# One transformer-like block on one core: seven block products in three of four token chunks, four of them summed by TensorE onto banks already read, and low parts of the probabilities on GpSimd

## The chip, the core and the metric

The kernel runs on one core of a Trainium2 chip. Its engines are TensorE (PE in the profile, with its weight loads as PEld), VectorE (DVE), ScalarE (ACT), GpSimd (POOL) and SyncE (SP), which issues the DMAs. The metric is device time in microseconds, the median over several runs of the program. Three runs of the kernel before took 1616.49, 1615.18 and 1614.28 us; the median is 1615.18 us.

## The reference

```python
x = A_x                                  # 1 x 2048 x 576
xn = _layernorm(x)
qkv = xn @ wqkv                          # 32 heads of 18; sliding window of 256 keys
p = softmax(mask(q @ k.T * 18 ** -0.5))
s = (p @ v) @ wo
g = silu(((xn @ w_gate) * (xn @ w_up)) @ w_down)    # 576 -> 4608 -> 576
return x + s * g
```

Everything is float32. The kernel keeps that precision by writing each number as a high and a low part in float16 and adding three products (high by high, high by low, low by high) for each wanted one.

## The kernel before, in words

**Stages.** A first stage normalizes x, turns it into XT (features on partitions, tokens along the free side: four blocks of 128 features and a tail of 64, each with high and low part), and computes q, k and v. The rest is one long loop of 72 slots (lines 1210 to 1232). A slot is a pair (g, c): g is one of 18 groups of 256 of the 4608 hidden features, c one of four chunks of 512 tokens, and c is the inner index. So chunk 2 comes in slots 2, 6, 10 and so on to 70. A slot does the gate and up products of its group for its chunk. Beside that, slot b carries one attention step s = b - 1 (64 steps: four chunks by sixteen pairs of heads), and the down projection of the slot before.

**Order.** A slot has 16 places. `at(slot, place, f, ...)` (line 547) writes a piece of work into a place, and `at_place` (550) issues it after the matmuls of that place. A place above 15 falls into the next slot. Every engine runs its own instructions in the order of issue, so the order is written out by hand. At one place score products come first, then the down projection, then all else in the order in which it was put there.

**A dense slot** (lines 1215 to 1231; chunks 2 and 3 before) does 13 passes of 512 tokens for each of four weight tiles `UW[g, k]` (52 matmuls at L1223) and two pairs of half passes (L1226, L1227) into the two PSUM banks named `up`. ACT copies the gate result out (`gate_out`, 922), DVE multiplies the up result with it into `ht` (`up_out`, 927).

**A seven slot** (chunks 0 and 1 before; `SEVEN`, line 418) splits the 2 x 2 x 2 block product of its tokens, features and inner blocks into seven products of half size instead of eight, in the manner of Strassen and Winograd. Products of sums need the sums of the weights (`t_sum`, 425, with `t_hi` and `t_lo`, 437 and 443: tiles `tf` and `tw`) and of the activations (`s_steps`, 451, made once for each chunk: tiles `sx`, `xd`, and one block of XT rewritten in place). `seven_place` (1060) issues 96 matmuls of 256 tokens (L1075), `SEVEN_N` (1117) of them in each place, and `seven_half` (1025) four half ones (L1031, L1033). Each product q gets a fresh `up` bank, of which there are two. `seven_read` (1089) reads a finished product: products 0, 3 and 4 are copied out by ACT (`seven_copy`, L1043), products 1, 2, 5 and 6 are read by DVE with an addition of an earlier sum (`seven_add`, L1047), three additions of two SBUF tiles go to POOL (`seven_sum`, L1051), and four multiplications of gate by up halves (`seven_mult`, L1057) go three to POOL and one to DVE.

**After the products**, in both kinds, ACT and DVE split `ht` into the high and low parts `hh` (`h_hi`, L934; `h_lo`, L939). The second `h_lo` comes at place 19 after a dense slot and at 21 after a seven slot, which are places 3 and 5 of the next one; the first comes at place 11 and at place 17. `down` (942) starts at place 7 of the next slot: eight rounds of six matmuls (L952) into the one bank `dn`, each added to `acc` by DVE (L957). Of the six, the last reads the low part of the second tile.

**Attention**: scores in PSUM (L826), row maximum and mask on DVE (L834, tile `sm`, four buffers), ACT shifts, exponentiates and casts the high part of P (L840, L844, L847), and `turn_probs` (852) subtracts to get the low part (L855). For the second head of a pair (j = 1) POOL does it; for the first head it is DVE, but in seven slots POOL does the blocks i = 1 and 3 (`PL_AT`, 850). Then SP issues a DMA that transposes P (L858, tile `pt`), and TensorE multiplies it with v (`weigh`, L867), seven to nine places later.

**Weights** of the next group are split in chunks 2 and 3 of this one and in chunk 0 of the next: `hi` on ACT (L152) and `lo` on DVE (L155), down weights also on POOL (L526).

## Time and profile before

| what | value |
|---|---|
| runs, median (lowest to highest) | 1615.18 us (1614.28 to 1616.49) |
| profiled execution: span from its first to its last instruction | 1611.0 us |
| granted TensorE clock in it | 1.000 |
| busy: DVE, ACT, POOL | 80%, 69%, 51% of the span |
| DMA queue of SP: share of 16 DMA engines | 63.7% |

Of the profiled execution the page gives the span and nothing around it. The median of the runs is 4.2 us above that span, which is start and end of the program. The profile has a page (busy time, slices of time, queues, the chain of work that ended last, the costliest groups of instructions) and views that answer questions: the waits, the chain piece by piece, the timeline, and busy times in windows. A row of the timeline is start, duration, engine, line, operation and tiles, and in brackets the idle time before it with what ended it. Matmul rows overlap, since matmuls are pipelined; the chain's rows do not.

### The profile page before, as it was taken

The numbers are of one execution on the slowest core, as the hardware profiler recorded it, in microseconds if no ns is written. First come the engines' busy times: TensorE is split into PE (matmuls) and PEld (weight loads), VectorE is DVE, ScalarE is ACT, GpSimd is POOL, SyncE is SP. The second block draws the span as 40 slices with busy tenths as digits, with TensorE's granted clock in tenths as the row PEclk, the third lists the DMA queues.
The fourth block names the chain that finished last, engine by engine and source line by source line (L and its number), as shares of the span: only waits on it lengthen the run. The fifth ranks groups of instructions, "written<-read, shape, count | busy, mean of one in ns | idle before, by whom it ended". The sixth has DMA issues, their size and how long they took to land.

```text
span 1611.0 us, 37834 instructions
## 1 busy us (share of the span) xinstructions
PE 1600.1 (99%) x13914; PEld 1086.2 (67%) x13914; DVE 1285.6 (80%) x3129; ACT 1117.7 (69%) x2211; POOL 827.5 (51%) x969
## 2 busy tenths in 40 slices
PE   8999999999999999999999999999999999999999
PEld 5464668576767676666767676767585757676677
DVE  7535788888888989898989898888888888976545
ACT  6433587878787878787878888887878787842230
POOL 3114456564746565656666656556565647453100
PEclk9999999999999999999999999999999999999999
DMA  9562445475656687777768686767686858660328
GB/s 237 172 188 88 128 83 126 95 130 97 130 107 127 134 135 132 128 142 124 151 117 151 111 157 112 152 113 153 112 155 114 156 116 152 118 132 1 61 74 221
DMA packets 548682, 206.70 MB, mean 128 GB/s; under 512 B 489360, under 2 KB 529296, under 8 KB 548496
## 3 DMA queue, kind: packets, MB, share of 16 engines
q1 hardware_dynamic: 548496, 204.28, 63.7%
q8 instruction: 109, 1.79, 0.5%
q14 instruction: 77, 0.63, 0.1%
HBM read 76.63 MB, written 23.75 MB: 62 GB/s over the span
## 4 chain that ended last, share of the span: by engine, by line
PE 96%; DMA 1%; DVE 1%; issue 1%; ACT 1%; SPq 0%; POOL 0%; POOLq 0%; DVEq 0%; ACTq 0%
PE up L1223 25%; PE dn L952 25%; PE up L1075 23%; PE pv L867 4%; PE s L342 3%; PE s L826 3%; PE s L952 2%; PE s L1185 2%; PE up L1185 1%; PE up L1226 1%; PE up L342 1%; PE s L293 1%; PE dn L342 1%; PE pv L342 1%; PE up L1031 1%
## 5 line engine op out<-in xcount | busy, mean ns | idle before, releaser
L952 PE MATMUL dn<-dnw,hh 128*128 128x288 f16 x3168 | 475.7, 286 | 0.0
L1223 PE MATMUL up<-XT,upw 128*128 128x512 f16 x1872 | 463.9, 378 | 0.0
L952 PEld LDWEIGHTS <-hh 128*128 128x128 f16 x3456 | 326.5, 98 | 155.5 <-issue 41.2
L957 DVE SCALAR_TENSOR_TENSOR acc<-dn,sc,acc 128x288 f32<-128x288 f32 x496 | 254.5, 513 | 146.0 <-PE dn L952 142.1
L840 ACT ACTIVATE mx<-mx,sig 128x1 f32<-128x1 f32 x512 | 193.3, 383 | 150.3 <-DVE mx L834 144.0
L1223 PEld LDWEIGHTS <-upw 128*128 128x128 f16 x1872 | 165.7, 97 | 138.7
L1075 PEld LDWEIGHTS <-upw 128*128 128x128 f16 x1728 | 163.8, 97 | 22.2 <-issue 1.1
L1075 PEld LDWEIGHTS <-tw 128*128 128x128 f16 x1728 | 156.4, 97 | 18.6 <-issue 1.1
L867 PEld LDWEIGHTS <-pt 128*128 128x128 f16 x2880 | 137.7, 96 | 38.1 <-DMA pt<-pp 0.4
L1075 PE MATMUL up<-XT,upw 128*128 128x256 f16 x1152 | 158.8, 272 | 0.5 <-DVE gt L1047 0.5
L1051 POOL TENSOR_TENSOR gt<-gt 128x512 f32<-128x512 f32 x108 | 137.9, 1277 | 15.7 <-ACT gt L1043 12.7
L867 PE MATMUL pv<-vt,pt 128*128 128x37 f16 x2880 | 142.9, 179 | 0.0
L934 ACT ACTIVATE hh<-ht 128x512 f16<-128x512 f32 x144 | 89.1, 619 | 76.4 <-POOL ht L1057 51.5
L886 POOL CAST ob<-o 128x144 f16<-128x144 f32 x64 | 19.5, 304 | 214.0 <-DVE o L882 214.0
L1075 PE MATMUL up<-sx,tw 128*128 128x256 f16 x864 | 126.4, 271 | 0.4 <-ACT gt L1043 0.4
L939 DVE SCALAR_TENSOR_TENSOR hh<-hh,ht 128x512 f16<-128x512 f16 x144 | 108.4, 753 | 13.9 <-ACT hh L934 13.0
L1075 PE MATMUL up<-XT,tw 128*128 128x256 f16 x864 | 111.7, 272 | 0.2 <-DVE gt L1047 0.2
L1047 DVE SCALAR_TENSOR_TENSOR gt<-up,gt 128x512 f32<-128x512 f32 x144 | 98.4, 683 | 6.1 <-PE up L1075 4.3
L1057 POOL TENSOR_TENSOR ht<-gt 128x256 f32<-128x256 f32 x108 | 89.9, 846 | 20.6 <-DVE gt L1047 17.7
L1043 ACT ACTIVATE gt<-up 128x512 f32<-128x512 f32 x108 | 63.0, 583 | 33.1 <-PE up L1075 25.6
L380 DVE TENSOR_REDUCE am<-raw 128x1 f32<-128x640 f32 (+1 forms) x108 | 83.9, 789 | 2.2 <-DMA raw<-in_B_w_gate_dram 1.6
L435 POOL TENSOR_TENSOR tf<-raw 128x256 f32<-128x256 f32 x72 | 68.7, 954 | 14.8 <-issue 7.4
(2289 smaller groups left out, 3035.5 us busy)
## 6 DMA issues: line engine op xcount, KB each, us to landing
raw<-in_B_w_down_dram SPq DMA_DIRECT2D x36, 288.0 KB
qk_d<-qp SPq DMA_DIRECT2D x18, 512.0 KB
raw<-in_B_w_gate_dram SPq DMA_DIRECT2D x36, 256.0 KB
raw<-in_B_w_up_dram SPq DMA_DIRECT2D x36, 256.0 KB
vt<-v_d SPq DMA_DIRECT2D x48, 111.0 KB
ks<-qk_d SPq DMA_DIRECT2D x96, 54.0 KB
v_d<-vo SPq DMA_DIRECT2D x16, 296.0 KB
xr<-in_A_x_dram SPq DMA_DIRECT2D x16, 288.0 KB
```

What stands on the lines that cost most here:

```text
L342: nc.tensor.matmul(ps, a, b, start=i == 0 and not opened, stop=i == 12 and opened)
L840: nc.scalar.activation(mx[:, 1:2], mx[:, 0:1], AF.Identity, bias=sig[:, 2:3], scale=sig[:, 1:2])
L867: nc.tensor.matmul(PVB[s][:, j, i, :VW], pt[:, 2 * nb * j + n], VT[s][:, lo_ + n % nb, j * VW:(j + 1) * VW], start=n == 0, stop=n == 2 * n ...
L934: nc.scalar.activation(hh[:, 0], h, AF.Copy, scale=1.0 / LO)
L939: nc.vector.scalar_tensor_tensor(hh[:, 1], hh[:, 0], -LO, h, op0=OP.mult, op1=OP.add)
L952: nc.tensor.matmul(ps[:, :HALF], a, b, start=q == 0, stop=q == len(l) - 1)
L957: nc.vector.scalar_tensor_tensor(d, ps[:, :HALF], SC[g][:, 9:10], d, op0=OP.mult, op1=OP.add)
L1047: nc.vector.scalar_tensor_tensor(seven_new(sl, name), CH[q], H_SC, x, op0=OP.mult, op1=OP.add)
L1051: nc.gpsimd.tensor_tensor(seven_new(sl, name), x, y, op=OP.add)
L1057: eng.tensor_tensor(HT[sl, f][:, 256 * i:256 * i + 256], u[:, 0:256], u[:, 256:512], op=OP.mult)
L1075: nc.tensor.matmul(CH[q][:, o], a, b, start=CH["n"] == 0, stop=last and q != 4)
L1223: nc.tensor.matmul(banks[up], a, b, start=i == 0 and not up, stop=i == 12 and up == 1)
```

## The change

- `SEVEN` becomes (0, 1, 2): chunk 2 goes from dense to seven slots, and gets its activation sums at places -10 to 14 around slot 0. Chunk 3 stays dense.
- The seven products come in the order 0, 2, 1, 3, 4, 5, 6. Products 1, 3, 5 and 6 get no fresh bank: TensorE adds them onto the bank of 0, 2, 3 and 4, after that bank has been read (`start=False`). What POOL's `seven_sum` added before is so added in PSUM, and `seven_sum` goes.
- The reads are now two copies by ACT (0 and 1) and five additions by DVE.
- `PL_AT` is (0, 1, 2, 3) in seven slots: POOL makes all low parts of P there.
- `t_hi` of the first two weight sums moves from place 45 to 47 and the first `t_lo` from 47 to 48, counted from the slot of chunk 0 of the group before.
- Since places of `h_hi`, `h_lo` and `score` depend on the kind of slot, chunk 2 now has those of a seven slot.

```diff
-    SEVEN = (0, 1)
+    SEVEN = (0, 1, 2)
...
+               (-10, -10, -9, -8, -6, -5, -4, 3, 4, 5, 6, 7, 8, 9, 10, 11, 13))
+    SUMS_ON = ("vvvvppvpvvpppvvvp", "ppppvpvpvvppvpvpv", "ppvvvpvpvvvpvpvpv")
...
-    PL_AT = ((), (1, 3))
+    PL_AT = ((), (0, 1, 2, 3))
...
-                at(b, (45, 45, 52, 57)[n], t_hi, g, n // 2, n % 2)
-                at(b, (47, 49, 56, 58)[n], t_lo, g, n // 2, n % 2)
+                at(b, (47, 47, 52, 57)[n], t_hi, g, n // 2, n % 2)
+                at(b, (48, 49, 56, 58)[n], t_lo, g, n // 2, n % 2)
...
-        CH[5], CH["n"] = bank("up", 2), 2
+        a, b = CH[4], CH[5]
...
-            nc.tensor.matmul(CH[5][:, o], w[64:128, 9], xh, start=kind == 0, stop=False)
+            nc.tensor.matmul(b[:, o], w[64:128, 9], xh, start=False, stop=False, skip_group_check=True)
...
-    def seven_sum(sl, x, y, name):
-        x, y = SV[sl, x], SV[sl, y]
-        nc.gpsimd.tensor_tensor(seven_new(sl, name), x, y, op=OP.add)
...
+    ORDER = (0, 2, 1, 3, 4, 5, 6)
+    ON = {1: 0, 3: 2, 5: 3, 6: 4}
...
+                q = CH["q"] = ORDER[CH["at"]]
+                CH["l"] = list(seven_unit(g, c, q))
+                CH[q] = CH[ON[q]] if q in ON else bank("up", 2)
+                CH["first"] = q not in ON
+                if q == 4:
+                    CH[5] = CH[3]
...
+            nc.tensor.matmul(CH[q][:, o], a, b, start=CH["first"], stop=last and q != 4, skip_group_check=q in ON)
...
         if q == 0:
             seven_copy(sl, 0, "t")
+        elif q == 2:
+            seven_add(sl, 2, "t", "u")
         elif q == 1:
-            seven_add(sl, 1, "t", "11")
+            seven_copy(sl, 1, "11")
             at(sl, place + 1, seven_mult, sl, "11", 0, 0, gp)
-        elif q == 2:
-            seven_add(sl, 2, "t", "t")
         elif q == 3:
-            seven_copy(sl, 3, "3")
-            at(sl, place + 1, seven_sum, sl, "3", "t", "3")
+            seven_add(sl, 3, "t", "v")
         elif q == 4:
-            seven_copy(sl, 4, "4")
-            at(sl, place + 1, seven_u4, sl)
-            at(sl, place + 3, seven_mult, sl, "4", 1, 1, gp)
+            seven_add(sl, 4, "v", "v")
+            at(sl, place + 1, seven_mult, sl, "v", 1, 1, gp)
         elif q == 5:
-            seven_add(sl, 5, "3", "11")
-            at(sl, place + 1, seven_mult, sl, "11", 1, 0, gp)
+            seven_add(sl, 5, "t", "t")
+            at(sl, place + 1, seven_mult, sl, "t", 1, 0, gp)
         else:
-            seven_add(sl, 6, "t", "t")
-            at(sl, place + 1, seven_mult, sl, "t", 0, 1, vec)
+            seven_add(sl, 6, "u", "u")
+            at(sl, place + 1, seven_mult, sl, "u", 0, 1, vec)
```

More of the change, by code (lines that the diff above doesn't have):

```diff
@@ L413, in up_lo @@
            w[:, 0:5])
[L418 to L419 removed]
+    SEVEN = (0, 1, 2)
     TF, TW, SX, XD = {}, {}, {}, {}
     def seven(sl):
[L423 removed]
+        return sl % NCH in SEVEN
     def t_sum(g, kind, pair, i):
```

26 lines of the change are left out of this document (7 added, 19 removed).

## The prediction, on record before the changed kernel ran

> **What bounds the kernel now.** I read the page's busy times and the shares of its chain of waits first, then the chain piece by piece over four slots in the steady middle (slots 40 to 43, chunks 0, 1, 2, 3), then the busy times in those four windows.
>
> ```profile
> span 1611.0 us, 37834 instructions
> PE 1600.1 (99%) x13914; PEld 1086.2 (67%) x13914; DVE 1285.6 (80%) x3129; ACT 1117.7 (69%) x2211; POOL 827.5 (51%) x969
> PE 96%; DMA 1%; DVE 1%; issue 1%; ACT 1%; SPq 0%; POOL 0%; POOLq 0%; DVEq 0%; ACTq 0%
> ```
>
> The busy 99% alone proves little, since matmul ends are modelled. The chain is the evidence: 96% of the span is matmul following matmul.
>
> ```profile
> 936.91 0.44 PE up L1075 x4
> 955.90 0.44 PE up L1075 x4
> 974.78 0.86 PE up L1223 x4
> 994.61 0.86 PE up L1223 x4
> 1014.43 0.44 PE up L1075 x4
> ```
>
> These rows are the first matmuls of five successive slots. Their distances are the slots' lengths: 18.99 us (chunk 0, seven), 18.88 (chunk 1, seven), 19.83 (chunk 2, dense), 19.82 (chunk 3, dense). Both kinds carry the same attention and down work. A seven slot has 96 matmuls of 256 columns at 0.44 / 4 = 0.11 us; a dense one has 52 of 512 at 0.86 / 4 = 0.215 us. So **one slot turned from dense to seven is worth 19.83 - 18.88 = 0.95 us, if nothing else makes TensorE wait**.
>
> ```profile
> 936.91:955.89 18.98, 18.98 (x207) 15.53 (x205) 17.33 (x42) 14.85 (x31) 12.29 (x13) 1.00 0.82 169
> 955.89:974.78 18.89, 18.89 (x206) 15.41 (x204) 15.66 (x42) 14.43 (x31) 13.16 (x15) 1.00 0.84 143
> 974.78:994.61 19.83, 19.83 (x162) 11.24 (x160) 15.09 (x44) 15.54 (x31) 11.58 (x16) 1.00 0.65 119
> 994.61:1014.43 19.82, 19.82 (x162) 11.28 (x161) 19.51 (x46) 18.27 (x36) 10.02 (x13) 1.00 0.71 113
> ```
>
> After the window come its length and the busy times of PE, PEld, DVE, ACT, POOL, then the clock. Chunk 2 has room on DVE (15.09 of 19.83). **Chunk 3 has none: 19.51 of 19.82 on DVE, 18.27 on ACT.** Whatever the change pushes there is what I have to look at.
>
> **The change part by part.** Prices of the operations:
>
> ```profile
> L1051 POOL TENSOR_TENSOR gt<-gt 128x512 f32<-128x512 f32 x108 | 137.9, 1277 | 15.7 <-ACT gt L1043 12.7
> L1047 DVE SCALAR_TENSOR_TENSOR gt<-up,gt 128x512 f32<-128x512 f32 x144 | 98.4, 683 | 6.1 <-PE up L1075 4.3
> L1057 POOL TENSOR_TENSOR ht<-gt 128x256 f32<-128x256 f32 x108 | 89.9, 846 | 20.6 <-DVE gt L1047 17.7
> L1043 ACT ACTIVATE gt<-up 128x512 f32<-128x512 f32 x108 | 63.0, 583 | 33.1 <-PE up L1075 25.6
> 975.41 0.55 DVE L855 TENSOR_TENSOR pp<-sm__15636,pp 128x384 f16<-128x384 f32 x1
> 976.35 0.47 DVE L1057 TENSOR_TENSOR ht<-gt 128x256 f32<-128x256 f32 x1
> 994.60 0.69 DVE L929 SCALAR_TENSOR_TENSOR ht<-up,gt 128x512 f32<-128x512 f32 x1
> 968.34 0.91 POOL L855 TENSOR_TENSOR pp<-sm__15501,pp 128x384 f16<-128x384 f32 x1
> ```
>
> *TensorE, chunk 2:* 18 slots by 0.95 us = **-17.1 us**.
>
> *Chunks 0 and 1, beside TensorE:* ACT loses one copy (-0.58), DVE gains an addition and loses two low parts (0.68 - 2 x 0.55 = -0.42), POOL loses three sums and gains two low parts (-3 x 1.28 + 2 x 0.91 = -2.0). All three get lighter beside a TensorE that stays as it is: worth 0 in the sum. At most it removes the 0.11 us by which chunk 0 is longer than chunk 1.
>
> *Chunk 2:* ACT has two copies either way. DVE gains five additions and a multiplication and loses two `up_out` and four low parts: 5 x 0.68 + 0.47 - 2 x 0.69 - 4 x 0.55 = +0.29, so about 15.4 of 18.9. POOL gains four low parts and three multiplications, 4 x 0.91 + 3 x 0.85 = +6.2, so 17.8 of 18.9, a part of it running over into chunk 3, which has 10.02. It is full but not over. Cost 0; if the cover were gone, the transposes would be late (a rival below).
>
> *The summing banks:* TensorE now waits for a read before it adds. Nearest is product 1 on the bank of 0: the twelve matmuls of product 2 (12 x 0.11 = 1.3 us) and a round of the down projection (0.73, row below) lie between, 2.0 us against ACT's 0.58 copy. Before, sixteen matmuls lay between. For products 3, 5 and 6 there are twelve to sixteen matmuls and one to two rounds, against DVE's 0.68. Behind such an addition DVE queues the `acc` addition that frees `dn`. I take 0; the bound is 0.3 us a seven slot if the reader is held up by its queue.
>
> *Chunk 3, the step that I price:* chunk 2 becomes a seven slot, so its first `h_lo` moves from its own place 11 to place 1 of chunk 3, and its second from place 3 of chunk 3 to place 5. DVE's total there barely grows: the multiplication and one more `h_lo` come (0.47 + 0.69), two low parts go (0.55 and more). But the second `h_lo` now stands at place 5 behind a weight split of the same place, and the down round at place 7 needs it.
>
> ```profile
> 1000.70 0.69 DVE L939 SCALAR_TENSOR_TENSOR hh<-hh,ht 128x512 f16<-128x512 f16 x1
> 1002.38 0.52 DVE L957 SCALAR_TENSOR_TENSOR acc<-dn,sc,acc 128x288 f32<-128x288 f32 x1
> 1002.77 0.73 POOL L435 TENSOR_TENSOR tf<-raw,tf 128x256 f32<-128x256 f32 x1
> 1002.81 1.36 DVE L155 SCALAR_TENSOR_TENSOR upw<-raw,sc,upw 128x640 f16<-128x640 f32 x1
> 1003.45 1.31 POOL L435 TENSOR_TENSOR tf<-raw 128x256 f32<-128x256 f32 x1
> 1003.79 0.73 PE dn L952 x6
> 1004.10 0.54 DVE L834 CUSTOM_DVE_ANT_0 sm__16165<-s,bias 128x384 f32<-128x384 f32 x1
> 1007.82 0.87 DVE L155 SCALAR_TENSOR_TENSOR upw<-raw,sc,upw 128x640 f16<-128x640 f32 x1
> 1019.95 1.11 DVE L939 SCALAR_TENSOR_TENSOR hh<-hh,ht 128x512 f16<-128x512 f16 x1
> ```
>
> Before, `h_lo` ran at 1000.70. In the new order DVE does L957 at 1002.38 (it had waited for TensorE, so this doesn't move), then the split at 1002.81, and from 1004.10, where the scores now stand, the `h_lo`: 1004.10 + 0.69 = 1004.79. TensorE starts that round at 1003.79 and its sixth matmul, the one that reads this part, 5 x 0.12 later at 1004.40. **It waits 0.4 us.** The split varies: 0.87 when POOL is quiet (1007.82), 1.36 when POOL works on its sums in those microseconds; `h_lo` 0.69 or 1.11. Ends of the range: 0.87 and 0.69 give 1004.3, no wait; 1.36 and 1.11 give 1005.2, 0.8 us. I take 0.4, since POOL, with more to do in chunk 2, will have its sums there no earlier. 16 slots of chunk 3 run beside attention: **+6.4 us** (0 to 13). What is late next, the `acc` addition of that round, has the 1.5 us of seven dense matmuls ahead of its next round and keeps.
>
> The Trainium skill, SBUF — State Buffer, Who interferes with whom, says that a DVE instruction with two SBUF inputs contends with a GpSimd instruction that reads SBUF, and that the later one blocks until the other is done. By that rule the split, which starts 0.04 us after a sum of POOL, would be held for the rest of that sum, 0.69 us, and the wait above would be some 0.6 us. The row shows 0.49 us (1.36 against 0.87), so the trace agrees in kind and the wait keeps the row's size.
>
> *Slots 0 and 1, once:* chunk 2's activation sums now fall into slots -1 and 0, on DVE, POOL and ACT.
>
> ```profile
> 151.37 1.16 POOL L469 TENSOR_TENSOR tf<-XT 128x512 f32<-128x512 f16 x1 [9.87 <-DVE xd L491]
> 152.56 0.69 DVE L469 TENSOR_TENSOR tf<-tf,XT 128x512 f32<-128x512 f32 x1 [1.32 <-POOL tf L469]
> 181.84 3.46 POOL L526 TENSOR_SCALAR dnw<-dnw 128x576 f16<-128x576 f16 x2 [0.26 <-ACT dnw L152]
> 182.29 1.47 PE L1075 MATMUL up<-sx,tw 128*128 128x256 f16 x12 [0.42 <-ACT gt L1043]
> 183.18 1.48 DVE L1047 SCALAR_TENSOR_TENSOR gt<-up,gt 128x512 f32<-128x512 f32 x2
> 183.91 1.47 PE L1075 MATMUL up<-XT,tw 128*128 128x256 f16 x12 [0.15 <-DVE gt L1047]
> ```
>
> TensorE waits here already (0.42, 0.15), because DVE and ACT come late out of the weight splits. In the new order DVE, after its read at 183.18, stands before a sum that waits for POOL (behind the first of two L526, 1.73, and a sum of 1.16: till 184.7), then ACT copies that sum before it copies product 1 (some 0.6 later than its bank is wanted, plus the sum's own 0.69). By this chain TensorE gets three waits of about 1.4, 0.7 and 0.7 us in slot 0 and loses the earlier ones: **+2 us** (0 to 4).
>
> *DMAs:* one small copy more; loads and transposes keep their places.
>
> **The sum:** -17.1 + 6.4 + 2 = -8.7 us; span 1602.3. The runs' median is 1615.18 - 1611.0 = 4.2 us above the profiled span, so 1606.5 us.
>
> **The rivals.**
>
> *Full gain.* The split in chunk 3 meets no POOL sum, slot 0 absorbs its sums, chunk 0 loses its 0.11 us: -17.1 - 18 x 0.11 + 1 = -18.1, so 1597 us. For it: DVE gets lighter in three chunks. Against it: the 19.51 in chunk 3.
>
> *Transposes late.* POOL is full in chunk 2 and runs in order; a low part behind its queue delays the DMA that transposes P.
>
> ```profile
> 995.01 1.47 SPq L858 DMA_TRANSPOSE pt<-pp  x1
> 1000.81 0.14 PE pv L867 x6
>   DMA pt<-pp: 0.4, 2
> ```
>
> The tightest transpose is issued 5.8 us before TensorE uses it; in all slots TensorE waited twice, 0.4 us together. So the margin is near zero there, and wider in the other blocks. If the queue makes one block of chunk 2 late by 0.5 us: 16 x 0.5 = +8 on the forecast, 1614 to 1615 us, no change. Against it: ACT makes the two heads' high parts over a microsecond apart, longer than POOL's 0.91.
>
> *Readers late.* The summing doesn't save the wait that it claims: TensorE stands before banks not yet read, 0.3 us in each of 54 seven slots: +16, 1622 us. Against it: chunk 1 shows no such wait now with the same two banks.
>
> *Slower: chunk 3's DVE.* One mechanism, at the round of place 7. If both the split and the `h_lo` stand behind whole POOL operations, the split behind a 1.31 sum (1002.81 + 1.31 + 0.87) and the `h_lo` at 1.11, it ends at 1006.1 and TensorE waits 1.7 us: 16 x 1.7 = 27 in place of 6.4, so 1627 us. It decides from (17.1 - 2) / 16 = 0.94 us a slot; above 1.15 the kernel is slower by over 0.2%. The SBUF rule named above speaks for it, as it lets each of these two meet an operation started earlier. The trace bears out single meetings, not two in a row: a chance of 1 in 10.
>
> **How the numbers follow.** Forecast (chunk 3 waits 0.1 to 0.8 us): 60%, 1599 to 1612. Full gain 14%, transposes late 10%, readers late 6%, slower in chunk 3 10%. A measurement of this kernel can tell about 0.2%, 3.2 us, from no change: under 1612 is faster, over 1618.4 slower. Forecast and full gain give 0.74, less 0.02 for the forecast's upper end; late transposes with that end 0.12; the last two 0.16. The range takes in the full gain with some play below it and leaves out the two slow cases: 1595 to 1617.
>
> **What would show it.** Right: chunk 2's slots at 18.9 to 19.0 us; chunk 3's at 20.2, with a gap ahead of the sixth matmul of its fourth down round, released by DVE's `hh` (L939); slot 0 some 2 us longer; L1051 gone, POOL near 17 us busy in chunk 2. Wrong: TensorE waiting for L1047 or L1043 in steady seven slots; waits for `pt`; chunk 3 at 19.8 (full gain) or above 20.8 (slower).

## The result and the profile after

The changed kernel takes **1621.68 us** (median of 4 runs, 1621.11 to 1624.99) against 1614.73 us for the kernel before on the same chip: a ratio of 1.0048, 95% interval 1.0035 to 1.006. It is slower by some 7 us, where 1606.5 us was forecast, with 1617 us as the upper end of the range. The profiled execution has a span of 1619.6 us, 8.6 more than before. Its own time is 1621.29 us, so start and end of the program take 1.7 us here; the 4.2 us that the median of the kernel before stood above its profiled span were more than that, which fits a profiled execution that was quicker than the median.

The page of the changed kernel, the rows that answer to those of before:

```profile
PE 1586.2 (98%) x14706; PEld 1164.2 (72%) x14706; DVE 1307.6 (81%) x3120; ACT 1115.0 (69%) x2180; POOL 818.3 (51%) x1050
...
PE 79%; DVE 12%; DMA 5%; issue 2%; POOL 1%; ACT 1%; SPq 0%; DVEq 0%; POOLq 0%; ACTq 0%
```

TensorE's busy time fell by 14 us and the kernel got slower, so TensorE waits more than it saved. The chain says on whom: DVE holds 12% of it, 1% before, and DMA 5%, 1% before; the largest DMA part is the one that spreads the scale of the next group's weights, for which DVE stands in some of chunk 2's slots (below). The busy shares of DVE, ACT and POOL hardly differ.

The same four windows as before (slots 40 to 43; columns as there: length, PE, PEld, DVE, ACT, POOL):

```profile
945.06:964.16 19.10, 19.05 (x207) 15.45 (x204) 17.33 (x42) 14.28 (x29) 12.15 (x14) 1.00 0.89 158
964.16:983.03 18.87, 18.87 (x207) 15.54 (x205) 15.35 (x41) 14.08 (x29) 10.08 (x14) 1.00 0.78 143
983.03:1001.93 18.90, 18.90 (x207) 15.56 (x205) 15.27 (x42) 15.53 (x31) 12.73 (x20) 1.00 1.06 133
1001.93:1022.63 20.70, 20.00 (x162) 11.23 (x160) 20.22 (x45) 19.11 (x37) 11.76 (x14) 1.00 0.55 100
```

Chunk 2 does what was forecast: 18.90 us for 19.83. Chunk 3 gives it back: 20.70 us for 19.82, with DVE busy 20.22 of it. For the whole kernel I took the start of the first matmul of each of the 72 slots in both traces and summed the differences of the slots' lengths by chunk (after less before): slot 0 +6.1, the other slots of chunk 0 -1.2, chunk 1 +2.3, **chunk 2 -14.7, chunk 3 +15.3**, head and tail +0.65; together +8.6, the difference of the spans.

The waits of TensorE in the changed kernel (total us, times, longest):

```profile
PE dn L952 <- DVE acc L957: 13.2, 18, 1.0
...
PE up L1075 <- DVE gt L1047: 3.0, 3, 1.7
PE up L1075 <- ACT gt L1043: 2.9, 2, 2.2
```

The first row is one kind of wait: a round of the down projection stands before its only bank, `dn`, until DVE has added the round before (L957). Fifteen of the 18 come once in each slot of chunk 3 from 7 to 63, together 11.0 us (slot 3's has a row of its own); the other three are in slots 18, 22 and 26 of chunk 2. Here is slot 43: the late round on TensorE and the fourth round, DVE's instructions up to them, and what POOL does beside them. The bracket is idle time before the instruction.

```profile
1007.29 0.90 PE L952 MATMUL dn<-dnw,hh 128*128 128x288 f16 x6 [0.70 <-DVE acc L957]
...
1011.86 1.02 PE L952 MATMUL dn<-dnw,hh 128*128 128x288 f16 x6
```

```profile
1000.82 1.47 DVE L155 SCALAR_TENSOR_TENSOR upw<-raw,sc,upw 128x640 f16<-128x640 f32 x1
1002.21 0.68 DVE L1047 SCALAR_TENSOR_TENSOR gt<-up,gt 128x512 f32<-128x512 f32 x1
1002.81 0.50 DVE L957 SCALAR_TENSOR_TENSOR acc<-dn,sc,acc 128x288 f32<-128x288 f32 x1
1003.23 1.20 DVE L155 SCALAR_TENSOR_TENSOR upw<-raw,sc,upw 128x640 f16<-128x640 f32 x1
...
1004.83 0.92 DVE L155 SCALAR_TENSOR_TENSOR tw<-tf,sc,tw 128x512 f16<-128x512 f32 x1
1005.67 1.13 DVE L1053 TENSOR_TENSOR ht<-gt 128x256 f32<-128x256 f32 x1
1006.73 0.51 DVE L957 SCALAR_TENSOR_TENSOR acc<-dn,sc,acc 128x288 f32<-128x288 f32 x1
...
1007.87 1.21 DVE L939 SCALAR_TENSOR_TENSOR hh<-hh,ht 128x512 f16<-128x512 f16 x1
```

```profile
1000.87 2.00 POOL L1053 TENSOR_TENSOR ht<-gt 128x256 f32<-128x256 f32 x2
1002.83 0.92 POOL L855 TENSOR_TENSOR pp<-sm__16402,pp 128x384 f16<-128x384 f32 x1
1003.71 1.50 POOL L855 TENSOR_TENSOR pp<-sm__16405,pp 128x384 f16<-128x384 f32 x1
1005.17 1.36 POOL L855 TENSOR_TENSOR pp<-sm__16432,pp 128x384 f16<-128x384 f32 x1
```

The same addition in slot 43 before the change:

```profile
998.03 0.51 DVE L957 SCALAR_TENSOR_TENSOR acc<-dn,sc,acc 128x288 f32<-128x288 f32 x1
```

That is 3.4 us after the slot's start (994.61); in the changed kernel it comes 4.8 us after it (1006.73 against 1001.93). DVE's queue has no gap here. The two up splits, the transposed-sum split and the multiplication all take longer than where POOL reads nothing beside them (0.87, 0.74 and, in e2 below, 0.41 us), each while POOL reads SBUF; L1047 and L957, which read PSUM, keep their 0.68 and 0.5 us. POOL is busy for 6.76 of the slot's first 7 us, where it was 4.12 before.

The late round is the **second** of the slot, by the count in which the prediction's is the fourth (the expectations below call it the third). Set side by side, the starts of slot 43's matmuls in both traces agree up to this round, which is 0.77 us late, and then differ by 0.11 us more at the sixth matmul of the fourth round, the one that reads `h_lo`: that round takes 1.02 us where the others take 0.90. Together they are the slot's 0.88 us.

In slot 22, as in 18 and 26, DVE stands at the reduction for the scale until its DMA has landed, and TensorE's round behind it is 1.0 us late (0.3 and 0.9 in the other two):

```profile
605.47 0.68 DVE L400 TENSOR_REDUCE sc<-tf 128x3 f32<-128x384 f32 x1 [0.94 <-DMA tf<-sd_f]
```

Slot 0, TensorE's waits and the piece of the chain between them:

```profile
182.44 0.61 PE L1075 MATMUL up<-sx,tw 128*128 128x256 f16 x4 [1.20 <-DVE tw L155]
...
183.75 1.91 PE L1075 MATMUL up<-XT,upw 128*128 128x256 f16 x16 [0.70 <-ACT gt L1043]
...
189.17 2.20 PE L1075 MATMUL up<-sx,tw 128*128 128x256 f16 x12 [2.21 <-ACT gt L1043]
```

```profile
183.30 2.30 POOL dnw L525
185.60 1.14 POOL tf L468
...
186.77 1.16 DVE tf L468
...
188.00 0.63 ACT sx L471
```

POOL's `dn_low` and a sum hold DVE's sum, that holds ACT's copy of it, and ACT's copy of product 1 (L1043) stands behind: the 2.21 us. After that wait the granted clock was 0.59 for 3.1 us, and the twelve matmuls took 2.20 us; in e6's trace the clock stays at 1.00 behind the same wait and the slot is as long, with longer waits later, so the clock is not what slot 0 loses by.

### The profile page after: what moved, and what is told of

It reads as the page before. It is cut to its first block, busy times and chain, and to the rows that moved or that the text cites. A ratio compares the mean times of both kernels' runs of the same rounds, so it can differ in the third digit from the quotient of the medians.

```text
span 1619.6 us, 39383 instructions
## 1 busy us (share of the span) xinstructions
PE 1586.2 (98%) x14706; PEld 1164.2 (72%) x14706; DVE 1307.6 (81%) x3120; ACT 1115.0 (69%) x2180; POOL 818.3 (51%) x1050
## 4 chain that ended last, share of the span: by engine, by line
PE 79%; DVE 12%; DMA 5%; issue 2%; POOL 1%; ACT 1%; SPq 0%; DVEq 0%; POOLq 0%; ACTq 0%
PE up L1075 27%; PE dn L952 21%; PE up L1216 10%; PE pv L867 3%; PE s L342 3%; DVE acc L957 2%; PE s L826 2%; DVE upw L155 2%; PE s L952 2%; PE s L1178 2%; PE up L1178 1%; DMA sd_f<-both 1%; PE up L342 1%; DVE gt L1047 1%; DVE ht L1053 1%
## 5 line engine op out<-in xcount | busy, mean ns | idle before, releaser
L957 DVE SCALAR_TENSOR_TENSOR acc<-dn,sc,acc 128x288 f32<-128x288 f32 x496 | 254.6, 513 | 136.0 <-PE dn L952 130.4
L1075 PEld LDWEIGHTS <-upw 128*128 128x128 f16 x2592 | 242.1, 97 | 33.1 <-issue 1.3
L1075 PEld LDWEIGHTS <-tw 128*128 128x128 f16 x2592 | 238.8, 97 | 32.9 <-issue 3.6
L1075 PE MATMUL up<-XT,upw 128*128 128x256 f16 x1728 | 253.9, 272 | 0.7 <-ACT gt L1043 0.7
L1216 PE MATMUL up<-XT,upw 128*128 128x512 f16 x936 | 232.0, 378 | 0.0
L1047 DVE SCALAR_TENSOR_TENSOR gt<-up,gt 128x512 f32<-128x512 f32 x270 | 184.7, 684 | 20.0 <-PE up L1075 16.5
L1053 POOL TENSOR_TENSOR ht<-gt 128x256 f32<-128x256 f32 x162 | 125.5, 788 | 125.8 <-ACT gt L1043 111.6
L1075 PE MATMUL up<-sx,tw 128*128 128x256 f16 x1296 | 175.6, 273 | 4.0 <-ACT gt L1043 2.2
L1075 PE MATMUL up<-XT,tw 128*128 128x256 f16 x1296 | 168.1, 273 | 0.0
L1216 PEld LDWEIGHTS <-upw 128*128 128x128 f16 x936 | 82.9, 97 | 68.9
L939 DVE SCALAR_TENSOR_TENSOR hh<-hh,ht 128x512 f16<-128x512 f16 x144 | 110.6, 768 | 0.0
L1043 ACT ACTIVATE gt<-up 128x512 f32<-128x512 f32 x108 | 63.5, 588 | 59.3 <-PE up L1075 58.2
L1075 PE MATMUL up<-sx,upw 128*128 128x256 f16 x648 | 88.2, 273 | 2.4 <-DVE gt L1047 2.4
L155 DVE SCALAR_TENSOR_TENSOR upw<-raw,sc,upw 128x640 f16<-128x640 f32 x72 | 76.7, 1065 | 0.3 <-ACT upw L152 0.3
```

Source lines behind the costliest of these rows:

```text
L155: nc.vector.scalar_tensor_tensor(w, rv, s, h, op0=OP.mult, op1=OP.subtract)
L939: nc.vector.scalar_tensor_tensor(hh[:, 1], hh[:, 0], -LO, h, op0=OP.mult, op1=OP.add)
L957: nc.vector.scalar_tensor_tensor(d, ps[:, :HALF], SC[g][:, 9:10], d, op0=OP.mult, op1=OP.add)
L1047: nc.vector.scalar_tensor_tensor(seven_new(sl, name), CH[q], H_SC, x, op0=OP.mult, op1=OP.add)
L1053: eng.tensor_tensor(HT[sl, f][:, 256 * i:256 * i + 256], u[:, 0:256], u[:, 256:512], op=OP.mult)
L1075: nc.tensor.matmul(CH[q][:, o], a, b, start=CH["first"], stop=last and q != 4, skip_group_check=q in ON)
```

## Experiments

All are edits of the changed kernel. In the table, each time is a median, beside that of the kernel before on the same chip, with the ratio's 95% interval; then, from each run's own trace, the differences to the kernel before as above (us, by slot 0, the other slots of chunk 0, and chunks 1 to 3).

| run | us | before | ratio | slot 0 | chunk 0 | chunk 1 | chunk 2 | chunk 3 |
|---|---|---|---|---|---|---|---|---|
| the change | 1621.68 | 1614.73 | 1.0035-1.006 | +6.1 | -1.2 | +2.3 | -14.7 | +15.3 |
| e1 low parts back | 1628.49 | 1613.31 | 1.0083-1.0111 | +6.1 | -1.2 | +2.5 | -11.2 | +19.8 |
| e2 no late low parts | 1604.93 | 1613.31 | 0.9942-0.9969 | +6.1 | -1.3 | +0.7 | -16.5 | +2.6 |
| e3 two chunks | 1618.77 | 1613.31 | 1.0023-1.0048 | +0.1 | -1.4 | +1.3 | 0.0 | +5.2 |
| e4 sums later | 1615.74 | 1613.31 | 1.0006-1.0023 | +1.3 | -1.2 | +1.8 | -16.2 | +15.2 |
| e5 tw back | 1623.28 | 1613.80 | 1.0045-1.0071 | +6.1 | -1.4 | +1.5 | -15.4 | +18.6 |
| e6 up early | 1635.93 | 1613.80 | 1.0118-1.0149 | +6.3 | -1.2 | +3.6 | +11.0 | +3.9 |
| e7 e4, e5, e6 | 1632.78 | 1613.80 | 1.0101-1.0129 | +1.3 | -1.3 | +3.2 | +11.6 | +3.9 |
| e8 e7 and more | 1657.80 | 1613.80 | 1.0255-1.0284 | +1.3 | -1.4 | +1.7 | +11.8 | +30.3 |
| e9 scale early | 1627.38 | 1614.03 | 1.0067-1.0094 | +1.3 | -1.4 | +2.9 | +7.9 | +5.0 |
| e10 tw late | 1627.51 | 1614.03 | 1.0069-1.0097 | +1.3 | -1.4 | +2.0 | -16.2 | +28.3 |
| e11 e9 and e10 | 1647.20 | 1614.03 | 1.0202-1.0233 | +1.3 | -1.4 | +3.8 | +1.6 | +28.3 |
| e12 scale at 37 | 1640.32 | 1612.08 | 1.0164-1.0191 | +1.3 | -1.3 | +1.7 | +21.6 | +5.0 |
| e13 sums of tw late | 1623.58 | 1612.08 | 1.0056-1.0084 | +1.3 | -1.4 | +3.5 | -16.7 | +23.5 |
| e14 mult on GpSimd | 1612.20 | 1614.18 | 0.9982-1.0 | +3.0 | -1.3 | +0.9 | -16.3 | +11.6 |
| e15 same, all chunks | 1613.07 | 1614.18 | 0.9981-0.9999 | +1.3 | -1.3 | +3.5 | -15.5 | +11.6 |
| e16 e14, split at 54 | 1598.82 | 1612.23 | 0.9904-0.9931 | +1.3 | -1.4 | +0.6 | -17.0 | +0.9 |
| e17 e14, split at 55 | 1598.19 | 1612.23 | 0.9897-0.9924 | +1.3 | -1.4 | +2.0 | -17.1 | -0.4 |

### Contention, or simply too much on DVE? (e1, e2, e3)

e1:

```diff
-    PL_AT = ((), (0, 1, 2, 3))
+    PL_AT = ((), (1, 3))
```

> The change with the low parts of P as before it (in the slots of seven products VectorE subtracts the first head's for the first and third row block, GpSimd the rest); all else as in the change. Contention theory (chunk 3's slots grew because GpSimd's reading instructions of the chunk before run into their first 8 us and lengthen VectorE's instructions with two SBUF inputs): one low part of 1.4 us leaves GpSimd there and 0.5 us comes to VectorE; VectorE's three L155 and its L1053 there shrink by 0.4 to 0.8 us in sum, so chunk 3 stands at 20.3 to 20.7 us a slot and the total at 1615 to 1621. Load theory (VectorE simply has more to do ahead of the third down round's addition, whatever GpSimd does): VectorE gets 0.5 us more, chunk 3 goes to 21.0 to 21.2 and the total to 1626 to 1631. In both chunk 2 stays at 18.9.

e2, in `turn_probs`, which leaves four low parts of P out of each of chunk 2's steps and writes zeros in their place:

```diff
-        (nc.gpsimd if j or i in PL_AT[seven(s + 1)] else nc.vector).tensor_tensor(...)
+        if seven(s + 1) and not seven(s + 2) and i > 1:
+            nc.gpsimd.memset(pp[:, a + n:a + 2 * n], 0.0)
+        else:
+            (nc.gpsimd if j or i in PL_AT[seven(s + 1)] else nc.vector).tensor_tensor(...)
```

> The change with the four last low parts of P of chunk 2's attention steps (row blocks 2 and 3, both heads: those that run in the first 8 us of chunk 3's slots) left out: GpSimd writes zeros there, which reads nothing. VectorE's instructions and their order are unchanged; output without those low parts. Contention theory: VectorE's L155 and L1053 in the first 6 us of chunk 3's slots go back towards the durations that they have alone (1.3 to 1.8 us less in sum), the wait for L957 ahead of the third down round goes, chunk 3 stands at 19.8 to 20.1 us a slot and the total at 1606 to 1612. Load theory: chunk 3 stays at 20.6 to 20.7 and the total at 1620 to 1622.

e3:

```diff
-    SEVEN = (0, 1, 2)
+    SEVEN = (0, 1)
```

> The change with the seven products in chunks 0 and 1 only, as before, and with its new order, its banks and all low parts on GpSimd; chunk 2 is dense again, and no sums of chunk 2's activations are made. Theory (the seven products of chunk 2 bring both the gain in chunk 2 and the loss in chunk 3): chunk 2 is back at 19.8, chunk 3 back at 19.8 us a slot. Rival (chunk 3's loss hangs on the all-GpSimd low parts or the later transposed weights): chunk 3 stays above 20.3. A dense chunk 2 behind a seven-product chunk 1 takes over the same inherited work, so by the contention theory chunk 2 may stand at up to 20.7 instead. Slot 0: if its 6.1 us come from the third chunk's activation sums, they fall to 0 to 2; if from the new order (the transform of the weights is needed a product earlier, and its first product is read by ScalarE), 3 to 6 remain. Total 1613 to 1620; 1629 to 1633 if chunk 2 takes 20.7.

**e2** hits the contention theory's numbers for chunk 3 and falls below its total (1604.93 us for 1606 to 1612): chunk 3 at 19.95 us in the window of slot 43, with the same 45 instructions on DVE, now 18.91 us busy instead of 20.22.

```profile
991.08:1011.03 19.95, 19.95 (x163) 11.16 (x161) 18.91 (x45) 18.85 (x37) 8.44 (x14) 1.00 0.58 106
```

Its timeline in that slot, DVE and POOL:

```profile
992.38 0.87 DVE L155 SCALAR_TENSOR_TENSOR upw<-raw,sc,upw 128x640 f16<-128x640 f32 x1
...
993.65 0.74 DVE L155 SCALAR_TENSOR_TENSOR tw<-tf,sc,tw 128x512 f16<-128x512 f32 x1
994.31 0.41 DVE L1056 TENSOR_TENSOR ht<-gt 128x256 f32<-128x256 f32 x1
...
991.96 1.13 POOL L856 MEMSET pp<- 128x384 f16 x3
```

And its multiplications over the whole kernel (times, busy us, mean ns):

```profile
L1056 DVE TENSOR_TENSOR ht<-gt 128x256 f32<-128x256 f32 x54 | 24.9, 460 | 0.0
```

(Lines of e2 are 3 higher from L856 on: its L1056 is L1053.) Beside POOL's three MEMSETs, which read nothing, the second up split takes 0.87 us, not 1.20; the multiplication, where a low part's subtraction no longer stands beside it, 0.41, not 1.13. Over the kernel, against the same row of the changed kernel,

```profile
L1053 DVE TENSOR_TENSOR ht<-gt 128x256 f32<-128x256 f32 x54 | 36.4, 674 | 0.0
```

the 54 of them lose 36.4 - 24.9 = 11.5 us. It is all in the 16 slots of chunk 3 beside attention: 1.13 us in each, 0.41 in e2. That one instruction's 0.72 us is about the length of the wait that e2 takes away; the second up split's 0.33 and the transposed-sum split's 0.18 come on top. What is left in e2's slot 43, 0.13 us, is at the sixth matmul of the fourth round.

The Trainium skill, SBUF — State Buffer, Who interferes with whom, says that a DVE instruction with two SBUF inputs contends with a GpSimd instruction that reads SBUF, and not with one that only writes it. By these rows the trace agrees: 1.20 us beside a subtraction, 0.87 beside MEMSETs, and nothing changed for L957 and L1047, which have one input in PSUM. In this stretch both sides get longer: GpSimd's L855 takes 1.50 and 1.36 us beside DVE's instructions, 0.92 at its shortest.

**e1** goes against the contention theory's number: chunk 3 gets longer, by 0.3 us a slot (20.98 us in slot 43, where the load theory put it), and so does chunk 2 (19.40 in slot 42, for 18.9 by both theories). One low part less on POOL doesn't pay for one more on DVE. The wait in slot 43:

```profile
1011.59 0.90 PE L952 MATMUL dn<-dnw,hh 128*128 128x288 f16 x6 [0.98 <-DVE acc L957]
```

So the low parts on GpSimd are the better of two places; both theories hold in part. DVE's queue counts, and contention is a good part of its length.

**e3** separates the rest: without chunk 2's seven products slot 0 keeps +0.1 and chunk 3 +0.3 us a slot (20.14 us, between the 19.8 and the 20.3 of the two expectations). By elimination the latter comes from the transposed-sum splits, the only edit that touches chunk 3 there (high parts at 47 for 45, the first low part at 48 for 47), which the prediction priced nowhere. The trace shows how:

```profile
998.01 1.54 DVE L155 SCALAR_TENSOR_TENSOR upw<-raw,sc,upw 128x640 f16<-128x640 f32 x1
...
997.55 1.32 POOL L855 TENSOR_TENSOR pp<-sm__15827,pp 128x384 f16<-128x384 f32 x1
```

Ahead of the second round's addition DVE has one transposed-sum split before and after. But ACT, which now makes the high parts later, casts P earlier, so a low part on POOL starts 1.2 us into the slot (3.0 before) and stands beside an up split, which takes 1.54 us for 0.88. Chunk 2 stands at before's 19.82, not at 20.7: a dense slot behind a seven slot isn't long by itself.

### Slot 0 (e4)

```diff
-               (-10, -10, -9, -8, -6, -5, -4, 3, 4, 5, 6, 7, 8, 9, 10, 11, 13))
+               (-10, -10, -9, -8, -6, -5, -4, 15, 16, 17, 18, 19, 20, 21, 22, 23, 25))
```

> The change with the ten last steps of chunk 2's activation sums twelve places later (places 15 to 25 in the place of 3 to 13: in the end of slot 0 and in slot 1); all else as in the change. Theory (slot 0's 6.1 us come from these steps, which stand ahead of the products' readers on ScalarE and VectorE and wait there for GpSimd): slot 0 loses 4 to 6 us, slot 1 grows by 0 to 1, total 1616 to 1618. Rival (they come from the new order of the products): slot 0 changes by less than 1.5 us, total 1620 to 1622.

Slot 0 falls from +6.1 to +1.3 us, slot 1 grows by 1.0 (-0.4 to +0.6), and the total lands at 1615.74. So the 4.8 us that went are the sums' queue across three engines. The order of the products is not what remains: e3 has it, and its slot 0 is at +0.1. In e4 the second product still waits 1.2 us for the split of the transposed sums (L155), in e3 0.5. Up to slot 0 the two differ in nothing but the first seven of chunk 2's sums, which e4 has there. The runs from e7 on carry this edit.

### Moving DVE's work in time (e5 to e13)

e5 and e6:

```diff
-                at(b, (47, 47, 52, 57)[n], t_hi, ...)
-                at(b, (48, 49, 56, 58)[n], t_lo, ...)
+                at(b, (45, 45, 52, 57)[n], t_hi, ...)
+                at(b, (47, 49, 56, 58)[n], t_lo, ...)
```

```diff
-  for k, (ph, pl) in enumerate(((43, 45), (44, 47), (49, 53), (55, 57))):
+  for k, (ph, pl) in enumerate(((41, 42), (42, 44), (44, 46), (55, 57))):
```

> The change with the high and low parts of the first transposed-sum weights at their old places (45, 45 and 47 in the place of 47, 47 and 48: in the end of chunk 2's slots rather than at the boundary and the start of chunk 3's). All else as in the change. With two chunks of seven products the change's remaining parts cost chunk 3 0.32 us a slot; this is the only edit that touches that slot there. Queue theory (that instruction of 0.8 us stands in VectorE's queue ahead of the addition that the third down round waits for): chunk 3 falls by 0.3 to 0.7, to 20.0 to 20.4 us a slot, total 1610 to 1616. Rival (VectorE's queue is full from the end of chunk 2's slot anyway, so that a step one place earlier changes nothing there): chunk 3 stays at 20.6 to 20.7, total 1620 to 1622.

> The change with three of the four splits of the next group's up weights in chunk 2's slots (high parts at places 41, 42, 44 and low parts at 42, 44, 46, in the place of 43, 44, 49 and 45, 47, 53): two VectorE instructions L155 of 1.1 us leave the first 6 us of chunk 3's slots, where VectorE's queue ends last; GpSimd's work is as in the change. Queue theory (what counts is how much stands in VectorE's queue there, its contention with GpSimd included): the wait of 0.8 us goes, chunk 3 stands at 19.8 to 20.0 us a slot, chunk 2 stays within 0.3 of 18.9, total 1606 to 1612. Rival (contention alone: GpSimd blocks VectorE for the length of its reading instructions, whichever of VectorE's instructions come): chunk 3 stays above 20.3, total 1615 or more.

e7 is e4 with both; e8 is e7 with the fourth split at `(47, 48)` and, in slot 69, `wo_in` at place 3 (6 before) and `wo_scale` at 13 (9).

> The three retimings together: the sums of chunk 2's activations twelve places later, the three up splits early and the first transposed-sum weights at their old places. Additive by the runs: 1621.7 less 6 (sums) less 13 (early splits) less 0 to 3 (the old places, when the wait is already gone) gives 1600 to 1604, faster than both kernels. Rival (the instructions moved into chunk 2 lengthen its slots by what chunk 3 loses): 1608 to 1614, with chunk 2 at 19.4 or more.

> As the run with the three retimings, with the fourth up split moved too (high part at place 47, low part at 48 in the place of 55 and 57) and, in slot 69, the spread of the output weights' scale asked for three places earlier and its reduction on VectorE four places later. If slot 69's extra 0.9 to 1.8 us come from VectorE standing at that reduction for the DMA, 1 to 2 us less than the run with the three retimings; the fourth split's move gives 0 to 2 us where chunk 3 still waits, and takes as much where it fills the boundary again: 1597 to 1604.

e5 missed: chunk 3 is longer by 0.2 us a slot, so the old places of the transposed-sum splits don't help in this kernel. e6 missed the total by 24 us, and shows why: chunk 3 does fall to 20.07 us, nearly as expected, but a round of *chunk 2* now waits 1.72 us, behind an up split of 1.59 us:

```profile
1009.07 1.59 DVE L155 SCALAR_TENSOR_TENSOR upw<-raw,sc,upw 128x640 f16<-128x640 f32 x1
...
1011.74 0.90 PE L952 MATMUL dn<-dnw,hh 128*128 128x288 f16 x6 [1.72 <-DVE acc L957]
```

```profile
991.69:1012.47 20.78, 19.06 (x206) 15.56 (x204) 17.07 (x44) 16.68 (x33) 14.11 (x20) 1.00 1.00 129
```

DVE is 17.07 us busy of 20.78 in that slot; it isn't full. It is late once, at one round, and that is enough. e7 repeats this with slot 0 mended; it and e8 miss the 1597 to 1614 us expected of them by far. In e8 both chunks wait, since the moved low part stands in DVE's queue for ACT's high part:

```profile
1029.12 0.91 DVE L155 SCALAR_TENSOR_TENSOR upw<-raw,sc,upw 128x640 f16<-128x640 f32 x1 [1.18 <-ACT upw L152]
```

The down round behind it waits 1.53 us. In e8 slot 69 is as in the kernel before, where the change had added 1.8 us; so that loss was DVE standing at the reduction (L1137) for the spread's DMA.

e9 moves the maxima and the scale of the next group's weights and the first two up splits into the half slot where DVE has gaps, e10 moves splits behind the second round, e11 does both (the edits in short):

```diff
-  ((9, 13) if g == 1 else (9, 9), (14, 26), (24, 29))    spread 30, 34   scale 40   up ((43, 45), (44, 47), ...
+  ((9, 13) if g == 1 else (9, 9), (14, 19), (18, 23))    spread 24, 28   scale 34   up ((35, 36), (37, 38), ...
```

```diff
-  t_sum (50, 51, 54, 55)   t_hi (47, 47, 52, 57)   t_lo (48, 49, 56, 58)
+  t_sum (53, 54, 54, 55)   t_hi (47, 47, 56, 57)   t_lo (52, 53, 58, 59)
```

> The change with the sums of chunk 2's activations twelve places later, and the preparation of the next group's weights six to ten places earlier: their maxima, the spread of the maxima and the scale (place 34 in the place of 40), and the splits of the first two up tiles (low parts at 36 and 38 in the place of 45 and 47); the other two splits stay. Those two and the scale then stand in the first half of chunk 2's slot, where VectorE has some 3 us of idle time, and leave its second half and the start of chunk 3's slot, where its queue has no gap for some 16 us. Backlog theory (the third down round of chunk 3 is late because VectorE enters the slot with a queue built up over the half slot before; what counts is when work is queued, not how much a slot holds): the wait goes, chunk 3 stands at 19.8 to 20.1 us, chunk 2 at 18.9 to 19.1, total 1600 to 1606. Rival (the contention with GpSimd fills whatever is freed, or the moved work makes its own queue in chunk 2 as the early splits did): chunk 3 at 20.4 or more, or chunk 2 at 19.4 or more; total 1612 to 1630.

> The change with the sums of chunk 2's activations twelve places later and, in chunk 3's slot, the low parts of the first transposed-sum weights at places 52 and 53 in the place of 48 and 49 (behind the third down round, not ahead of it), GpSimd's sums for the second ones at 53 to 55 in the place of 50 to 55, and their splits accordingly later (56 to 59). Backlog theory: 0.9 to 1.7 us of VectorE's queue and 2 us of GpSimd's reads leave the stretch ahead of the third round; the wait of 0.8 us goes: chunk 3 at 19.8 to 20.1 us, total 1600 to 1606. Rival (VectorE is simply full in chunk 3's slot, 20.0 us busy of 20.7, so that work moved within the slot is late at a later round): chunk 3 at 20.4 to 20.7, total 1611 to 1616.

> Both of the retimings before, with the later sums. If each alone already takes the wait of the third round away, the two together give no more than one (1600 to 1606), less what later rounds of chunk 3 still waited (0.1 to 0.2 us a slot, 2 to 3 us); if each takes half, 1602 and the sum of both. Rival (each makes a new queue of its own): above both, 1610 or more.

```profile
DVE sc L400 <- DMA tf<-sd_f: 16.6, 16, 3.0
```

```profile
1014.28 0.30 PE L952 MATMUL dn<-dnw,hh 128*128 128x288 f16 x1 [1.11 <-DVE hh L939]
```

In e9 chunk 3 comes to 20.00 us, but the scale (L400) now stands in DVE's queue until its DMA has landed, up to 3.0 us, and chunk 2 pays. In e10 the second round's wait is gone, but the *fourth* round waits 1.11 us for `h_lo` (L939), behind a split moved ahead of it, and the eighth 0.26 us; its total lies above both expectations. e11 has both faults.

e12 puts the scale of e9 at 37, the splits at `((37, 38), (38, 40), ...`, with e8's edit for slot 69; e13 moves only GpSimd's sums out of the stretch ahead of the second and fourth rounds, with the splits that need them:

```diff
-  t_sum (50, 51, 54, 55)   t_hi (47, 47, 52, 57)   t_lo (48, 49, 56, 58)
+  t_sum (53, 54, 54, 55)   t_hi (47, 47, 56, 57)   t_lo (48, 49, 57, 58)
```

> The change with chunk 2's activation sums twelve places later, the maxima and the spread of the next group's weights as early as in the run with the early scale, but the scale itself at place 37 (there 34, where VectorE waited up to 3.0 us for the DMA of the spread; in the change 40) and the low parts of the first two up splits at 38 and 40 (in the change 45 and 47), and slot 69's spread of the output weights' scale asked for earlier and reduced later. Backlog theory: with the DMA landed in time chunk 2 stays at 18.9 to 19.1 and chunk 3 at 19.9 to 20.1 us a slot, slot 69 loses 1 to 2 us: total 1600 to 1606, faster than both kernels. Rival (the queue on VectorE only moves): chunk 2 at 19.4 or more, total 1612 or more.

> The change with chunk 2's activation sums twelve places later and, in chunk 3's slots, GpSimd's two sums L434 for the second transposed weights at places 53 and 54 in the place of 50 and 51 (their splits follow, from 52 and 56 to 56 and 57); nothing on VectorE ahead of the third and fourth down rounds is moved, only GpSimd's reads of 0.9 and 1.1 us go from that stretch. Against the run with the later sums alone (1615.7). Contention theory: VectorE's instructions there (L155, L939) shorten by 0.3 to 0.8 us, chunk 3 stands 0.2 to 0.6 below 20.7, total 1606 to 1613. Rival (VectorE's own work alone sets the third round): no change in chunk 3, total 1614 to 1617.

```profile
1005.00 1.60 DVE L155 SCALAR_TENSOR_TENSOR upw<-raw,sc,upw 128x640 f16<-128x640 f32 x1 [0.59 <-ACT upw L152]
```

```profile
1008.52 0.68 DVE L939 SCALAR_TENSOR_TENSOR hh<-hh,ht 128x512 f16<-128x512 f16 x1
...
1012.55 1.22 DVE L939 SCALAR_TENSOR_TENSOR hh<-hh,ht 128x512 f16<-128x512 f16 x1
...
1011.08 2.14 POOL L434 TENSOR_TENSOR tf<-raw,tf 128x256 f32<-128x256 f32 x2
...
1013.83 0.30 PE L952 MATMUL dn<-dnw,hh 128*128 128x288 f16 x1 [0.48 <-DVE hh L939]
```

e12 (first fence) mends the DMA's wait and meets the old two faults instead, a split that waits for ACT and then takes 1.60 us beside GpSimd; chunk 2's round behind it is 0.87 us late, one of four waits in that slot. e13 (second) missed: it took the contention from the first `h_lo` (0.68 us; 1.21 in the changed kernel) and gave it to the second (1.22; 0.69 there), whose round then waits. The second round's 0.70 us stays, since the sums had stood behind it. That DVE's two `h_lo` change their times with GpSimd's sums is a second sign of the contention.

### Taking work out of DVE's chain (e14 to e17)

```diff
-            at(sl, place + 1, seven_mult, sl, "u", 0, 1, vec)
+            at(sl, place + 1, seven_mult, sl, "u", 0, 1, gp if sl % NCH == 2 else vec)
```

with e4's and e8's edits for slots 0 and 69; e15 has `gp` in all three chunks.

> The change with chunk 2's activation sums twelve places later, slot 69's spread of the output weights' scale asked for earlier and reduced later, and the last product of two halves (L1053, of the seventh block product) of chunk 2's slots on GpSimd in the place of VectorE. It is the instruction right ahead of the addition that the third down round of chunk 3 waits for (1.13 us there, 0.47 alone; GpSimd's own take 0.73 alone). Chain theory: VectorE's addition comes 1.1 us sooner, the wait of 0.7 to 0.9 us goes: chunk 3 at 19.8 to 20.1 us a slot, chunk 2 unchanged, slot 69 1 to 2 us less, total 1599 to 1606, faster than both kernels. Rival (GpSimd's longer stretch of reads lengthens VectorE's L155 and L939 by as much, or the product comes so late on GpSimd, behind four low parts, that h_hi and h_lo are late for the fourth round): chunk 3 at 20.4 to 21.5, total 1610 to 1628.

> As the run before, with that product on GpSimd in the slots of all three chunks of seven products. Chunks 0 and 1 wait for nothing steadily on VectorE, so by the chain theory they don't change, and the total is that of the run before within 3 us; if the product is late on GpSimd there, their slots grow by 0.2 us or more each and the total by 7 us or more.

```profile
1004.42 0.88 DVE L155 SCALAR_TENSOR_TENSOR upw<-raw,sc,upw 128x640 f16<-128x640 f32 x1
1005.21 1.22 DVE L939 SCALAR_TENSOR_TENSOR hh<-hh,ht 128x512 f16<-128x512 f16 x1
...
1006.49 0.30 PE L952 MATMUL dn<-dnw,hh 128*128 128x288 f16 x1 [0.48 <-DVE hh L939]
```

The second round's wait is gone, as the chain theory has it, but chunk 3 gains 0.2 us a slot and not 0.8. What is left is one wait, 0.48 us, ahead of a single matmul of the fourth round: `h_lo` behind the third up split. **This is the very wait that the prediction priced, at 0.4 us.** In the changed kernel the second round's wait had covered it but for 0.11 us. e15's time equals e14's within 1 us, and its seven slots show no steady wait for the multiplication on POOL, only single ones. (In e14's profile slot 0 is 1.7 us longer than in e15's, with TensorE at a granted clock of 0.88.)

e16 moves the third up split one place later, behind `h_lo`, e17 two places:

```diff
-  ((43, 45), (44, 47), (49, 53), (55, 57))
+  ((43, 45), (44, 47), (49, 54), (55, 57))
```

> The run with chunk 2's last product of halves on GpSimd, and in chunk 3's slot the low part of the third up split one place later (54 in the place of 53), so that h_lo (L939) stands ahead of this L155 in VectorE's queue and not behind it. In that run only one wait of TensorE was left in chunk 3: 0.48 us in slot 43 (0.5 to 0.7 over all) at the fourth down round, for this L939, which started as the L155 of 0.88 us ended. Chain theory: L939 starts 0.8 us earlier, the wait goes, chunk 3 stands at 19.8 to 20.0 us a slot (there 20.5), total 1600 to 1606, faster than both kernels. Rival (as in the five retimings before, the moved L155 makes a later round wait): chunk 3 at 20.4 or more, total 1611 or more.

> As the run before, two places later instead of one (55 in the place of 53). By the chain theory the same within 0.1 us a slot where the fifth round's addition has slack, 0.1 to 0.4 us a slot more where the L155 now stands ahead of that addition and of the product of halves L929.

e17, the chain of its page:

```profile
PE 93%; DMA 2%; DVE 2%; ACT 1%; issue 1%; SPq 1%; POOL 0%; POOLq 0%; DVEq 0%; ACTq 0%
```

Slot 43's window, and in its timeline `h_lo` in its new place:

```profile
986.59:1006.41 19.82, 19.82 (x162) 11.23 (x160) 19.46 (x44) 18.39 (x36) 13.35 (x15) 1.00 0.58 105
```

```profile
994.95 0.74 DVE L939 SCALAR_TENSOR_TENSOR hh<-hh,ht 128x512 f16<-128x512 f16 x1
```

Chunk 3 is back at 19.82 us, chunk 2 stays at 18.9, and the kernel takes **1598.19 us** (0.9911 of the kernel before, 0.9897 to 0.9924): faster than both kernels, by four edits that leave the change's products as they are: the sums of chunk 2 later, slot 69's reduction later, one multiplication on GpSimd, one split two places later. DVE is 19.46 us busy of 19.82 in that window, as full as before the change: fullness alone doesn't make TensorE wait.

## Why the prediction was wrong

- **Chunk 2, -17.1: right.** 0.92 to 0.96 us a slot. The changed kernel shows -14.7, mostly because three slots (18, 22, 26) lost 0.3 to 1.0 us each to a single wait, behind DVE standing for the scale's DMA; e16 and e17 show -17.0 and -17.1.
- **Chunks 0 and 1, 0: nearly right.** Chunk 0 gains the 0.11 us a slot that was named as the most, from slot 20 on (-1.2). Slot 69's +1.8, at the reduction for the output weights, wasn't seen (e8); the rest of chunk 1 is mostly one slot (25, +0.74) in which TensorE waits for a transpose; such single waits fall elsewhere in other runs.
- **The summing banks, 0: right.** No steady wait for L1047 or L1043; the 5.9 us of both are five waits, four in slots 0 and 1 and one in slot 69, behind the reduction just named. The rival of late readers falls.
- **Chunk 3, +6.4: this step failed.** It measured +15.3, 0.88 us a slot for 0.4. The step priced one round, the fourth, by one instruction that moves behind another, and took DVE's time before it from the old trace: "L957 at 1002.38 ... doesn't move". It did move, because TensorE's second round was already 0.77 us late: DVE came out of chunk 2's slot with a queue that has no gap, and its instructions in that queue took longer beside GpSimd's work left over from chunk 2. The up splits took 1.47 and 1.20 us (0.87 alone), the transposed-sum split 0.92 (0.74), and chunk 2's multiplication, new in chunk 3's slots, 1.13 (0.41 in e2). The step said of DVE that its "total there barely grows"; the number of instructions does not, their durations do. Without GpSimd's reads (e2) or without the multiplication (e14) the second round is on time.
- **POOL in chunk 2, cost 0.** "Near 17 us busy" was named as a sign of being right; it is 12.73 (11.58 before). The prediction did say that a part would run over into chunk 3, but not what it would do to DVE's durations there: that is what the step above left out.
- **The priced wait itself** was real and of the priced size (0.48 us, e14), but stood second in line, and the size is in part luck: the split was priced at 1.36 us and `h_lo` at 0.69, and they took 0.88 and 1.22.
- **Slots 0 and 1, +2: wrong size.** 6.1 - 0.4 = 5.7 us. The mechanism was right (e4): TensorE waits 2.21 us for the copy of product 1, where 1.4 was priced, since POOL's `dn_low` took 2.30 us, not 1.73. The 1.2 us before it, for the split of the transposed sums, was left out.
- **The sum of terms** would have been -14.7 + 15.3 + 5.7, and 1.5 for the rest of chunks 0 and 1, in place of -8.7; head and tail add 0.65. Of the 4.2 us added for the runs' median, 2.1 were there (1621.68 - 1619.6).
- **The rivals.** The slower one, DVE held by whole POOL operations in chunk 3, had the right cause, GpSimd's reads beside DVE, with a chance of 1 in 10. Its price was 1.7 us a slot; the measured 0.88 is just under the 0.94 that it named for a tie, and slot 0's missing 3.7 us did the rest. Its place was off, the fourth round for the second. Late transposes: TensorE's weight loads and matmuls waited for one six times, 2.3 us together, of which a matmul once, 0.57 us: not the bound. The full gain, 1597 us, is what e16 and e17 reach once the queue is mended.

Two things stay open. e2 removes both GpSimd's reads and 3.3 us of its time. That DVE waited for none of GpSimd's results there is read from the waits, not tried apart. And of e3's 0.3 us a slot it is not shown how much is still in the changed kernel, where the old places of the splits (e5) make chunk 3 longer.

## What to carry to other kernels

Where one engine must empty a single bank every second step, read its queue round by round: what decides is which addition is latest, not how full the engine is (e6 was late at 82% busy, e17 on time at 98%). When work moves, price the queue that it enters from the slot before, with durations as they are beside the instructions that will then run next to it; and when the named wait goes, look for the next one behind it, as it was hidden and not absent. In e5 to e13 moves in time only handed the wait on; taking an instruction out of the chain (e14), and then putting what the consumer needs first (e16), removed it.

## What the runs showed of the hardware

- DVE's multiplication of two SBUF tiles takes 0.41 us in slot 43 of e2 and 1.13 us in the changed kernel beside GpSimd's subtractions, nearly three times as long; GpSimd's subtraction takes 0.92 to 1.50 us in that slot. An up split on DVE beside GpSimd's MEMSETs takes 0.87 us, as it does alone.
- DVE's instructions with an input in PSUM keep their time beside all of these: over the changed kernel L957 takes 0.50 to 0.52 us, L1047 0.68 to 0.69 us.
- A split that stood on DVE for ACT's half for 1.18 us (e8) was followed by a wait of 1.53 us on TensorE, and a reduction that stood there 3.0 us for a DMA (e9) by one of 2.19 us, since a down round's addition was queued behind each.
